# Hash-masked attention and a SwiGLU layer in one kernel: the normed rows of five half batches turned by transposing DMAs

## Chip, core and metric

The kernel runs on one core of a Trainium2 chip. The metric is the device time of one launch in microseconds (us). Of the kernel before, three runs gave 341.06, 342.76 and 345.58 us, a median of 342.76 us.

## What is computed

Four batches, eight heads, 768 tokens, head size 64. Each query and key gets a bucket of six sign bits, a query sees only the keys of its own bucket, and the attention's output (3072 rows of 512) goes through an RMS norm and a SwiGLU layer with 1536 hidden columns.

```python
q_bucket = sum((q @ proj > 0) * 2 ** arange(6)); k_bucket = the same of k
scores   = where(q_bucket == k_bucket, q @ k.T / sqrt(64), -1e9)
attn_out = softmax(scores) @ v                       # 4 x 8 x 768 x 64
x   = attn_out.transpose(0, 2, 1, 3).reshape(3072, 512)
xn  = x / sqrt(mean(x * x) + 1e-6) * rms_g           # rms_g: 512 numbers
g   = xn @ w_gate                                    # 512 x 1536
out = (g * sigmoid(g) * (xn @ w_val)) @ w_out        # 1536 x 512, float32
```

## The kernel before

The work is cut into eight half batches, w = 0 to 7, of 384 rows each, and for the attention into 192 slots: one slot is one third of the keys of one head of one half batch. In slot s the kernel issues the score matmuls of slot s + 1 on TensorE (`scores`, L323) and their exponential on ScalarE (`probs`, L333). Everything else hangs on a hand-written plan: `at(s, f, ..., rank=r)` puts a piece of work into slot s, and within a slot work of rank under 3 comes before the exponential and the rest behind it, in order of rank. No scheduler reorders anything, so each engine does its work in the order of the plan, and an instruction that waits holds up all that stands behind it on its engine.

For a half batch w of 2 or more, the last attention matmul stands in slot end = 24w + 26, and the feed-forward part begins with `g_step` in slot s0 = 24w + 48, which is end + 22. The part in between prepares the rows:

- `attn_out` (L360 to L381): VectorE adds a small mean to the attention output and takes reciprocals, GpSimd multiplies (x) and squares (sq). `sumsq` (L385, VectorE) sums the squares.
- `norm` (L392 to L398), in slot end + 9: VectorE adds the four sums of a row, GpSimd makes 1/sqrt of the mean (rstd).
- `scale_x` (L403), in slots end + 14, 15 and 16, one for each third c of the 384 rows: VectorE multiplies 128 rows of x by rstd and writes them as fp16 (xn).
- `turn_x` (L410, L411), in slots end + 17, 19 and 21: TensorE transposes the 128 rows in four 128x128 pieces into a PSUM bank (x_ps), and VectorE moves the bank to xnT and multiplies by the norm's weight, which lies there as a column (gcol).

Then come, from slot s0 on, twelve pairs of `gate` (L422, TensorE; tanh L424, ScalarE) and `value` (L432, TensorE; L434 and L435, VectorE) in sixteen slots, and `project` (L446) in the nine slots behind them. So while half batch w is being normed, TensorE is at the pairs and the projection of half batch w - 1, and the attention of half batch w + 1 runs through all slots. x_ps, the two banks of a pair, and the projection's bank come from one pool of three PSUM banks (`gps`).

SyncE issues nearly all DMAs, in the order of the plan: the loads of q, k and v of the next heads (L121 in four pieces each for q and k, L111 for v), the moves of the hash bits from SBUF to SBUF (L288, eight for two pairs of heads), and the outputs (L455). The DMAs take eight completion semaphores in turn, so a DMA can't be issued before the one eight places earlier has landed. `v_sum` (L301 to L303, GpSimd) adds the six blocks of v in a scratch tile.

Of the kernel before, what the change touches and what calls it, by code (L numbers as in the profile page):

```python
# [8 lines left out]
FP32 = mybir.dt.float32  # L9
FP16 = mybir.dt.float16  # L10
AF = mybir.ActivationFunctionType
ALU = mybir.AluOpType
# [5 lines left out]
D = 64  # L18
DMODEL = H * D
# [7 lines left out]
KBIT = -32.0  # L27
ESCALE = 1.0 / 8.0
C0 = 1.0e-9

# [11 lines left out]
def kernel(  # L44
# [12 lines left out]
    nc = tc.nc  # L57
    PSUM = bass.MemoryType.PSUM

    const = ctx.enter_context(tc.tile_pool(name="const", bufs=1))  # L60
# [7 lines left out]
    spool = ctx.enter_context(tc.tile_pool(name="spool", bufs=2))  # L68
# [13 lines left out]
    scl = const.tile([128, 1], FP32, name="scl")  # L82
    mhalf = const.tile([128, 3], FP32, name="mhalf")
    gcol = const.tile([128, 4], FP32, name="gcol")
    wg = const.tile([128, 4, DFF], FP16, name="wg")
    wv = const.tile([128, 4, DFF], FP16, name="wv")
    wo = const.tile([128, NF, DMODEL], FP16, name="wo")
    vls = [const.tile([128, H, 6, 66], FP16, name=f"vl{i}") for i in range(2)]
    vsum = [const.tile([128, H, 66], FP16, name=f"vsum{i}") for i in range(2)]
    cvb = [const.tile([128, H, 66], FP32, name=f"cvb{i}") for i in range(2)]  # L90

    def bank(name, shape=None, dt=FP32):
        return gps.tile(shape or [128, 512], dt, name=name, tag="g")
# [203 lines left out]
    def v_sum(b, hp):  # L297
        vn = raw[b, hp, "v"]
        hs = slice(2 * hp, 2 * hp + 2)
        a = spool.tile([128, 2, 3, D], FP32, name="vadd")  # L300
        nc.gpsimd.tensor_add(a, vn[:, :, 0:3], vn[:, :, 3:6])  # L301
        nc.gpsimd.tensor_add(a[:, :, 0], a[:, :, 0], a[:, :, 1])
        nc.gpsimd.tensor_add(vsum[b % 2][:, hs, 0:64], a[:, :, 0], a[:, :, 2])  # L303

    def v_mean(b, hp, n, parts=(None,)):
        hs = slice(2 * hp, 2 * hp + n)
        ps = bank("m_ps", [128, n, 65])
        for i, jt in enumerate(parts):
# [3 lines left out]
            )  # L312
        nc.vector.tensor_scalar_mul(cvb[b % 2][:, hs, 0:65], ps, C0 / S)  # L313


    sps, psb, ot = {}, {}, {}
    x, ssp, xn, xnT, ht = {}, {}, {}, {}, {}
# [70 lines left out]
    rstds = {}  # L388
# [11 lines left out]
    def scale_x(w, c):  # L400
        if w not in xn:
            xn[w] = npool.tile([128, 3, DMODEL], FP16, name="xn")
        nc.vector.tensor_scalar_mul(xn[w][:, c, :], x[w][:, c, :], rstds[w][:, c : c + 1])  # L403

    def turn_x(w, c):
        if w not in xnT:
            xnT[w] = npool.tile([128, 4, HALF], FP16, name="xnT", bufs=2)
        ps = bank("x_ps", [128, 4, 128], FP16)
        for kt in range(4):
            nc.tensor.transpose(ps[:, kt, :], xn[w][:, c, kt * 128 : (kt + 1) * 128], ident16)  # L410
        nc.vector.tensor_mul(  # L411
            xnT[w][:, :, c * 128 : (c + 1) * 128], ps,
            gcol.unsqueeze(2).to_broadcast([128, 4, 128]),
        )
# [88 lines left out]
    def load_wo(f0, f1):  # L503
        nc.gpsimd.dma_start(
            out=wo[:, f0:f1, :],
            in_=moe_w_out[f0 * 128 : f1 * 128, :].rearrange("(k p) n -> p k n", p=128),
        )

    def columns_of_proj():
# [40 lines left out]
    def at(s, f, *a, rank=3):  # L550
        plan[s].append((rank, len(plan[s]), lambda: f(*a)))
# [36 lines left out]
    for i, (t, src) in enumerate(((wg, moe_w_gate), (wv, moe_w_val))):  # L588
        at(2 + 4 * i, load_w, t, src, 0, 768)
        at(12 + 5 * i, load_w, t, src, 768, 1536)  # L590
        at(33 + 6 * i, load_wo, 6 * i, 6 * i + 6)
# [26 lines left out]
    for (b, hp), (loads, turns, cast_slots, sh) in work.items():  # L618
        for which, s in zip("kqv", loads):
            at(s, load_rows if which == "v" else load_blocks, nc.sync, b, hp, which)  # L620
        for i, s in enumerate(turns):
            at(s, turn_dve, b, hp, "kq"[i // 4], i % 4, rank=5)
        for which, s in zip("kq", cast_slots):
            at(s, cast_pool, b, hp, which)
        if sh:
            at(sh, hash_pairs, b, (hp,) if b == 1 else (hp - 1, hp))
        at(cast_slots[2], v_prep, b, hp)
        at(cast_slots[2], v_sum, b, hp)
        if hp % 2:
            at(64 if b == 1 else 48 * b - 4 + 4 * hp, v_mean, b, hp - 1, 4)  # L630
    for hp in range(2):
        at(52 + 4 * hp, v_mean, 1, hp, 2, range(6))

    gts, sqs = {}, {}

    def g_step(w, ft):
# [12 lines left out]
    for w in range(8):  # L649
        for h in range(H):  # L650
            end = LAST[w, h] + 3
            at(end - 1, av, w, h, 0, 9)
            at(end, av, w, h, 9, 18)
            if h % 2:
                at(end, o_step, w, h // 2, rank=4.5)
                if (w, h) != (0, 7):
                    at(end + 6, s_step, w, h // 2, rank=5)
        at(end + (1 if w == 0 else 9), norm, w, rank=5)
        for c in range(3):
            at(end + (3 if w == 0 else 14 + c), scale_x, w, c, rank=5)  # L660
            at(end + (7 + c if w == 0 else 17 + 2 * c), turn_x, w, c, rank=1)
        s0 = 24 * w + 48
        seen = set()
        for ft in range(NF):
            for f, s in ((g_step, s0 + 16 * ft // NF), (v_step, s0 + (32 * ft + 16) // (2 * NF))):
                at(s, f, w, ft, rank=4 if s in seen else 2)
                seen.add(s)
        for i in range(9 if w < 7 else 6):
            c, j = divmod(i, 3)
            at(s0 + 16 + i, project, w, c, 4 * j, 4 * j + 4, rank=1 if i == 8 else 3)  # L670


    for s in range(NS + 48):
# [3 lines left out]
        n = sum(r < 3 for r, _, _ in todo) if s < NS - 1 else 0  # L677
# [54 lines left out]
```

## Time and profile before

| | |
|---|---|
| median of three runs | 342.76 us |
| the profiled execution: its own time | 343.48 us |
| its span in the trace | 341.7 us (1.8 us lie around it) |
| TensorE (PE) busy | 330.2 us, 97% of the span |
| VectorE (DVE) busy | 238.6 us, 70% |
| ScalarE (ACT) busy | 210.2 us, 62% |
| GpSimd (POOL) busy | 150.6 us, 44% |
| granted TensorE clock, mean | 0.995 |

In the lines of the profile, L410 is a line of the kernel before; then come engine, operation, what is written and what is read, with tile sizes, and "x96" is the number of instructions. Behind the bar stand the busy time, the mean of one in nanoseconds, and how long the engine had been idle before them and for whom. PEld is TensorE's loading of weights, which runs beside its matmuls. "SPq" and "POOLq" are queue instructions, the issue of a DMA among them.

### The profile page before, as it was taken

The numbers are of one execution on the slowest core, as the hardware profiler recorded it, in microseconds if no ns is written. First come the engines' busy times: TensorE is split into PE (matmuls) and PEld (weight loads), VectorE is DVE, ScalarE is ACT, GpSimd is POOL, SyncE is SP. The second block draws the span as 40 slices with busy tenths as digits, with TensorE's granted clock in tenths as the row PEclk, the third lists the DMA queues.
The fourth block names the chain that finished last, engine by engine and source line by source line (L and its number), as shares of the span: only waits on it lengthen the run. The fifth ranks groups of instructions, "written<-read, shape, count | busy, mean of one in ns | idle before, by whom it ended". The sixth has DMA issues, their size and how long they took to land.

```text
span 341.7 us, 7760 instructions
## 1 busy us (share of the span) xinstructions
PE 330.2 (97%) x2985; PEld 200.8 (59%) x2985; DVE 238.6 (70%) x530; ACT 210.2 (62%) x328; POOL 150.6 (44%) x222
## 2 busy tenths in 40 slices
PE   8899998999999999999999999999999999999995
PEld 5366665665556565566565666566556655555553
DVE  3577888898759896668668896667446663883860
ACT  3588987756667576657666676567667674322421
POOL 3668897636464667244746475503111311110000
PEclk9899999999999999999999999999999999999999
DMA  6999999635557064507344251100010001002002
GB/s 203 353 175 220 253 186 165 106 84 107 97 148 133 13 107 117 109 17 135 97 101 91 43 115 63 35 16 0 33 63 0 3 2 73 18 2 83 12 0 92
DMA packets 80100, 31.36 MB, mean 92 GB/s; under 512 B 65192, under 2 KB 77120, under 8 KB 80064
## 3 DMA queue, kind: packets, MB, share of 16 engines
q1 hardware_dynamic: 76160, 26.09, 31.1%
q0 software_dynamic: 3680, 4.72, 8.6%
q8 instruction: 23, 0.38, 0.4%
q14 instruction: 13, 0.11, 0.1%
q10 hardware_dynamic: 224, 0.07, 0.1%
HBM read 28.32 MB, written 6.29 MB: 101 GB/s over the span
## 4 chain that ended last, share of the span: by engine, by line
PE 87%; DVE 8%; POOL 1%; issue 1%; ACT 1%; DVEq 0%; ACTq 0%
PE v_ps L432 18%; PE y_ps L446 18%; PE g_ps L422 17%; PE s_ps L323 16%; PE o_ps L345 9%; PE d_ps L209 5%; PE x_ps L410 1%; DVE otmp L360 1%; PE t_ps L169 1%; PE z_ps L491 1%; POOL QK L185 1%; PE y_ps L689 1%; DVE xn L403 1%; DVE ssp L385 1%; PE m_ps L310 1%
## 5 line engine op out<-in xcount | busy, mean ns | idle before, releaser
L333 ACT ACTIVATE psb<-s_ps 128x768 f16<-128x768 f32 x192 | 150.8, 809 | 30.5 <-PE s_ps L323 29.5
L323 PE MATMUL s_ps<-QK 76*128 76x384 f16 x384 | 93.7, 326 | 2.8 <-ACT psb L333 1.1
L424 ACT ACTIVATE t<-g_ps 128x384 f32<-128x384 f32 x96 | 47.2, 492 | 62.2 <-PE g_ps L422 62.0
L432 PE MATMUL v_ps<-xnT,wv 128*128 128x384 f16 x384 | 78.0, 325 | 0.9 <-DVE cvb L313 0.5
L422 PE MATMUL g_ps<-xnT,wg 128*128 128x384 f16 x384 | 78.0, 325 | 0.4 <-DVE xnT L411 0.4
L434 DVE SCALAR_TENSOR_TENSOR a<-t,g_ps 128x384 f32<-128x384 f32 x96 | 52.7, 549 | 27.9 <-ACT t L424 26.1
L446 PE MATMUL y_ps<-wo,ht 128*128 128x512 f16 x276 | 69.2, 378 | 0.5 <-DVE a L434 0.5
L369 POOL TENSOR_TENSOR x<-otmp,rcp 128x384 f32<-128x384 f32 x31 | 25.8, 832 | 95.6 <-DVE rcp L365 95.3
L345 PEld LDWEIGHTS <-psb 128*128 128x128 f16 x1152 | 51.7, 98 | 25.2 <-issue 7.5
L435 DVE SCALAR_TENSOR_TENSOR ht<-a,v_ps 128x384 f16<-128x384 f32 x96 | 53.2, 554 | 11.4 <-PE v_ps L432 2.2
L345 PE MATMUL o_ps<-vl,psb 128*128 128x65 f16 x1152 | 56.8, 193 | 0.4 <-DVE otmp L360 0.4
L432 PEld LDWEIGHTS <-wv 128*128 128x128 f16 x384 | 36.3, 97 | 25.4 <-issue 1.7
L422 PEld LDWEIGHTS <-wg 128*128 128x128 f16 x384 | 35.9, 97 | 24.3 <-issue 0.6
L323 PEld LDWEIGHTS <-QK 76*128 76x128 f16 x384 | 31.6, 98 | 18.5 <-issue 4.9
L446 PEld LDWEIGHTS <-ht 128*128 128x128 f16 x276 | 25.8, 97 | 24.3 <-issue 0.6
L453 ACT COPY ysb<-y_ps 128x512 f32<-128x512 f32 x23 | 13.5, 587 | 25.4 <-PE y_ps L446 22.6
L411 DVE TENSOR_TENSOR xnT<-x_ps,gcol 128x512 f16<-128x512 f16 x24 | 16.3, 685 | 15.9 <-PE x_ps L410 15.9
L381 POOL TENSOR_TENSOR sq<-x 128x384 f32<-128x384 f32 x31 | 25.6, 827 | 2.4
L360 DVE TENSOR_TENSOR otmp<-o_ps,cvb 128x390 f32<-128x390 f32 x32 | 17.9, 558 | 10.3 <-PE o_ps L345 10.3
L201 POOL CAST QK<-kT 64x768 f16<-64x768 f32 x20 | 16.7, 836 | 13.5 <-DVE kT L193 6.5
L216 DVE TENSOR_SCALAR bits<-d_ps,thr,scl 128x384 f16<-128x384 f32 (+1 forms) x20 | 13.3, 675 | 12.4 <-PE d_ps L209 12.3
L201 POOL CAST QK<-qT 64x768 f16<-64x768 f32 x20 | 16.7, 836 | 9.2 <-DVE qT L193 8.6
(74 smaller groups left out, 284.2 us busy)
## 6 DMA issues: line engine op xcount, KB each, us to landing
vL<-in_v_dram SPq DMA_DIRECT2D x16, 384.0 KB
out_dram<-ysb SPq DMA_DIRECT2D x23, 256.0 KB
kL<-in_k_dram SPq DMA_DIRECT2D x40, 96.0 KB
qL<-in_q_dram SPq DMA_DIRECT2D x40, 96.0 KB
kL<-in_k_dram SPq DMA_DIRECT2D x5, 384.0 KB
qL<-in_q_dram SPq DMA_DIRECT2D x5, 384.0 KB
wg<-in_moe_w_gate_dram POOLq DMA_DIRECT2D x2, 768.0 KB, 7.2
wv<-in_moe_w_val_dram POOLq DMA_DIRECT2D x2, 768.0 KB, 9.0
```

Source lines behind the costliest of these rows:

```text
L201: nc.gpsimd.tensor_copy(QK[b, hp][0:64, hh, o : o + S], T0[b, hp, which][64 * hh : 64 * hh + 64, :])
L323: nc.tensor.matmul(ps[:, j, 0:HALF], k_cols(w // 2, h, 2 * p + j), q_cols(w, h), start=True, stop=True,)
L333: nc.scalar.activation(psb[w, h][:, p], sps.pop(g)[:, :, 0:HALF], AF.Exp, scale=ESCALE,)
L345: nc.tensor.matmul(o[:, c, hh, 0:65], psb[w, h][:, jt // 2, jt % 2, 128 * c : 128 * c + 128], vls[b % 2][:, h, v_chunk(b, h, jt), 0:65], s ...
L369: eng.tensor_mul(xd.rearrange("p c (h d) -> p c h d", h=2), tmp[:, :, :, 0:64], r.to_broadcast([128, 3, 2, 64]),)
L381: nc.gpsimd.tensor_mul(sq, xd, xd)
L422: nc.tensor.matmul(g, wg[:, kt, fs], xnT[w][:, kt], start=(kt == 0), stop=(kt == 3))
L424: nc.scalar.activation(t, g, AF.Tanh, scale=0.5)
L432: nc.tensor.matmul(vv, wv[:, kt, fs], xnT[w][:, kt], start=(kt == 0), stop=(kt == 3))
L434: nc.vector.scalar_tensor_tensor(out=a, in0=t, scalar=1.0, in1=g, op0=ALU.add, op1=ALU.mult)
L435: nc.vector.scalar_tensor_tensor(out=ht[w][:, ft], in0=a, scalar=0.5, in1=vv, op0=ALU.mult, op1=ALU.mult)
L446: nc.tensor.matmul(y, ht[w][:, ft, c * 128 : (c + 1) * 128], wo[:, ft, :], start=(ft == 0), stop=(ft == NF - 1),)
```

## The change

Half batches 2 to 6 no longer use TensorE for the turn. VectorE multiplies x by rstd and by the norm's weight in one instruction, for which the weight is loaded once as a row copied to all partitions (grow). Then SyncE issues twelve transposing DMAs for each of these half batches, each 128x128 fp16 from xn to xnT. In their plan `norm` stands in slot end + 7, and `scale_x` and `turn_x` of third c both in slot end + 11 + c, the latter at rank 6, behind the slot's other work. Half batches 0, 1 and 7 are as before. `v_sum` forms its sum in a smaller scratch tile, which with one buffer instead of two makes room for grow.

```diff
+BY_DMA = (2, 3, 4, 5, 6)
+    grow = const.tile([128, DMODEL], FP32, name="grow")
 def v_sum(b, hp):
-        a = spool.tile([128, 2, 3, D], FP32, name="vadd")
-        nc.gpsimd.tensor_add(a, vn[:, :, 0:3], vn[:, :, 3:6])
-        nc.gpsimd.tensor_add(a[:, :, 0], a[:, :, 0], a[:, :, 1])
-        nc.gpsimd.tensor_add(vsum[b % 2][:, hs, 0:64], a[:, :, 0], a[:, :, 2])
+        a = spool.tile([128, 2, 2, D], FP32, name="vadd", bufs=1)
+        nc.gpsimd.tensor_add(a, vn[:, :, 0:2], vn[:, :, 2:4])
+        nc.gpsimd.tensor_add(a, a, vn[:, :, 4:6])
+        nc.gpsimd.tensor_add(vsum[b % 2][:, hs, 0:64], a[:, :, 0], a[:, :, 1])
 def scale_x(w, c):
-        nc.vector.tensor_scalar_mul(xn[w][:, c, :], x[w][:, c, :], rstds[w][:, c : c + 1])
+        if w in BY_DMA:
+            nc.vector.scalar_tensor_tensor(
+                out=xn[w][:, c, :], in0=x[w][:, c, :], scalar=rstds[w][:, c : c + 1],
+                in1=grow, op0=ALU.mult, op1=ALU.mult,
+            )
+        else:
+            nc.vector.tensor_scalar_mul(xn[w][:, c, :], x[w][:, c, :], rstds[w][:, c : c + 1])
 def turn_x(w, c):
+        if w in BY_DMA:
+            for kt in range(4):
+                nc.sync.dma_start(
+                    out=xnT[w][:, kt, c * 128 : (c + 1) * 128],
+                    in_=xn[w][:, c, kt * 128 : (kt + 1) * 128], transpose=True,
+                )
+            return
+    def load_grow():
+        nc.sync.dma_start(
+            out=grow, in_=moe_rms_g.rearrange("(o n) -> o n", o=1).to_broadcast([128, DMODEL])
+        )
+    at(63, load_grow)
-        at(end + (1 if w == 0 else 9), norm, w, rank=5)
+        at(end + (1 if w == 0 else 7 if w in BY_DMA else 9), norm, w, rank=5)
         for c in range(3):
-            at(end + (3 if w == 0 else 14 + c), scale_x, w, c, rank=5)
-            at(end + (7 + c if w == 0 else 17 + 2 * c), turn_x, w, c, rank=1)
+            scale, turn, rank = (3, 7 + c, 1) if w == 0 else (14 + c, 17 + 2 * c, 1)
+            if w in BY_DMA:
+                scale, turn, rank = 11 + c, 11 + c, 6
+            at(end + scale, scale_x, w, c, rank=5)
+            at(end + turn, turn_x, w, c, rank=rank)
```

## The prediction

> **What bounds the kernel now.** I read the page's first part, then the waits, then the timeline around one turn.
>
> ```profile
> PE 330.2 (97%) x2985; PEld 200.8 (59%) x2985; DVE 238.6 (70%) x530; ACT 210.2 (62%) x328; POOL 150.6 (44%) x222
> PE 87%; DVE 8%; POOL 1%; issue 1%; ACT 1%; DVEq 0%; ACTq 0%
> ```
>
> TensorE is busy 97% of the span and makes 87% of the chain that ended last. Between 58 and 290 us the view of the waits gives it 1.4 us of waiting in all. So what shortens the kernel is TensorE work taken away, and what lengthens it is any wait of TensorE. VectorE, ScalarE, GpSimd and SyncE have room on the average, but the room at the places touched must be read there. The timeline of TensorE at the projection of half batch 2:
>
> ```profile
> 166.12 0.49 PE L323 MATMUL s_ps<-QK 76*128 76x384 f16 x2
> 166.44 1.03 PE L446 MATMUL y_ps<-wo,ht 128*128 128x512 f16 x4
> 167.31 0.49 PE L323 MATMUL s_ps<-QK 76*128 76x384 f16 x2
> 167.63 0.39 PE L410 MATMUL x_ps<-ident,xn 128*128 128x128 f16 x4
> 167.86 1.03 PE L446 MATMUL y_ps<-wo,ht 128*128 128x512 f16 x4
> ```
>
> Columns: start, duration (us). Matmuls overlap, so the cost of a turn is read from starts: without one, y_ps starts 0.32 us after s_ps; with one, 0.55 us after it. A turn of four transposes costs TensorE 0.23 us, though the groups give L410 9.3 us for 96.
>
> **What goes.** Five half batches of three turns: 15 x 0.23 = 3.4 us of TensorE. The chain, which holds x_ps at 1.4% of the span (4.8 us for 24 turns), gives 15/24 of it, 3.0 us. I take 3.4. The built order confirms 60 weight loads and 60 matmuls fewer on TensorE. VectorE loses 15 evictions:
>
> ```profile
> L411 DVE TENSOR_TENSOR xnT<-x_ps,gcol 128x512 f16<-128x512 f16 x24 | 16.3, 685 | 15.9 <-PE x_ps L410 15.9
> L403 DVE TENSOR_SCALAR xn<-x,rstd 128x512 f16<-128x512 f32 x24 | 14.8, 652 | 0.0
> ```
>
> 15 x 0.685 = 10.3 us, off the path, and 15 uses of the three PSUM banks, for which TensorE hardly waits.
>
> **What the scaling costs.** It gets a second SBUF input. Rows of the same operation: 279 ns for 128 columns (L376), 553 for 384 (L434), so 1.07 ns per column and 0.69 us for 512, against 0.65 now: 0.6 us over 15, and VectorE gains 9.7 in all. But it moves three slots forward, from the projection's slots into the last pairs. There VectorE is nearly full: 7.26 of the 8 us from 118 to 126. For half batch 2:
>
> ```profile
> 122.05 0.55 DVE L434 SCALAR_TENSOR_TENSOR a<-t,g_ps 128x384 f32<-128x384 f32 x1
> 122.71 0.55 DVE L435 SCALAR_TENSOR_TENSOR ht<-a,v_ps 128x384 f16<-128x384 f32 x1
> ```
>
> The first projection's matmul starts at 124.59 and takes the bank that this L435 leaves at 123.26; with three banks the slack is 1.3 us. The value matmul before it, at 123.61, takes the bank of this L434, left at 122.60: 1.0 us. Two of three scalings come ahead by then, 1.4 us, less 0.3 us that VectorE idled. So TensorE waits 0 to 0.4 us. Half batch 3 shows the same pairs (161.5 to 163.5), 4 is alike, and in 5 and 6 VectorE idles 0.4 to 0.95 us between pairs. I take 0.8 us in all; nothing if the slack holds, 3 x 2.07 = 6.2 us if all three scalings reach TensorE each time.
>
> GpSimd: `v_sum` was 996 + 458 + 457 ns. At (996 - 458)/256 = 2.1 ns per column, 256 columns take 0.73 us, and 0.73 + 0.73 + 0.46 is the same 1.9. The norm two slots earlier finds GpSimd idle (2.1 us before L394 at 120.00). grow is one more issue at slot 63 (0.34 to 0.71 us by the rows below), 22 slots ahead of its first use.
>
> **What the transposing DMAs cost.** No row shows one. Two numbers matter: I, how long one keeps SyncE (or the rings) before the next goes, and L, its landing. SyncE's own rows give medians for I of 338 ns (outputs), 492 (v), 644 (pieces of q and k) and 714 (bits). The upper end is far: the longest single issue of a piece took 2,513. The bits are the nearest, the only moves from SBUF to SBUF, so I take 0.71. L, from timelines of SyncE and GpSimd:
>
> ```profile
> 117.53 3.20 SPq L288 DMA_DIRECT2D QK<-bits  x4
> 120.83 2.69 SPq L121 DMA_DIRECT2D kL<-in_k_dram  x4
> 123.57 2.71 SPq L121 DMA_DIRECT2D qL<-in_q_dram  x4
> ...
> 122.08 1.70 POOL L201 CAST QK<-kT 64x768 f16<-64x768 f32 x2 [0.93 <-DMA QK<-bits]
> ```
>
> The last bits are issued by 120.73 and release GpSimd at 122.08: L = 1.35, taken as 1.4 (first load of the trace, from HBM: 2.9).
>
> Now the cover, half batch by half batch, in times of the trace before, with the gate 0.68 us earlier (three turns less). Half batch 2: the scores of slot 85 start at 120.13, but SyncE is late: it had waited for the bits, and the q pieces that the plan puts ahead of the transposes go out until 126.28. The gate starts at 137.36 - 0.68 = 136.68. So 136.68 - 126.28 - 1.4 = 9.0 us are left for twelve issues: 12 x 0.71 = 8.5 fits, by half a microsecond, and I = 0.75 is the limit. For the others the start is the first scaling's end, or SyncE's freedom if later (161.8; 198.9 plus a v load of 0.64; 237.4; 273.9), the gates 176.26, 214.34, 252.67 and 288.48, less 0.68: covers of 12.4, 12.7, 13.2 and 12.5 us, limits of I of 1.03 to 1.1. The last scaling comes at least 8 slots ahead of the gate and its four transposes follow it, so it doesn't bind. If the cover fails, TensorE stands for 12 I minus the cover, each time.
>
> Behind the transposes on SyncE wait v loads (for half batch 2 needed 12 slots later, at slot 100), outputs and pieces of q and k of slots 90 to 98. A delay of 8.5 us leaves the pieces ahead of their turns on VectorE in slot 106. The output of slot 90 goes out some 6 us later, and with two ysb buffers ScalarE's third copy may wait under 1 us, once; I leave it at nothing, since ScalarE idles 62 us before the tanh. The eight semaphores bind only if a landing takes over 8 x 0.71 = 5.7 us.
>
> **Sum.** -3.4 + 0.8 + 0 = -2.6 on the profiled execution's own 343.48: 340.9 us, -0.8%. The median of the runs is 0.7 lower than that execution, within their spread of 4.5, so I shift nothing.
>
> **A rule against it.** The trace moves a SBUF-to-SBUF piece every 0.71 us. The Trainium skill, "VectorE: DVE Perf Modes", section "The three transpose paths", gives 1309 ns for a 128x128 transpose by DMA and 390 by TensorE, and advises TensorE where PSUM will do; no run here shows that figure. By it, I = 1.31, the waits would be an estimated 6.7 + 3.3 + 3.0 + 2.5 + 3.2 = 18.7 us and the time 359.6, within the second case of the first rival below. "Advanced Engine Details and Errata", section "X-Bar Transpose (TRN2)", says instead that such DMAs are as fast as regular ones, which agrees with my choice.
>
> **Rivals.**
> *Transposes too slow for the cover* (slower). From I = 0.75 half batch 2 waits, from 1.03 the others too. With I twice the bits' row, 1.43, 12 I = 17.1 and the waits are 8.1 + 4.7 + 4.4 + 3.9 + 4.6 = 25.7: 366.6 us. With 2.51, 30.2: 91 us, 432. It passes +2% (349.6) at about I = 1.14. For it: 65,192 of the 80,100 DMA packets are under 512 B and rows of 256 B are such, and the rings are busy 0.84 to 1.06 from 123 to 129 us, just ahead of the first transposes. Against it: they are idle from 131 to 134 and the dearest median row is 0.71. Chance of I between 0.75 and 1.14: 0.12 (341 to 349.6); to 1.43: 0.14 (to 366.6); above: 0.14.
> *VectorE becomes the bound in the last pairs of half batches 2 to 4*: up to 6.2 - 3.4 = +2.8, 346.3 us. For it the 91% there, against it the slack of 1.0 to 1.3 us. 0.07.
> *More gain than the transposes themselves*: to pass -2% it would take 6.9 us, and TensorE's waits outside the first 10 us hold too little. 0.03.
> *Nothing is moved*: excluded by the built order.
>
> **Numbers.** The forecast, with 338.5 to 343.5 of its own, has 0.50. 2% is about what a measurement of this kernel tells from no change. Within it: 0.50 + 0.12 + 0.07 = 0.69; slower 0.28; faster 0.03. The range goes from 338.5 to 366 and leaves out the slowest rival and the fast one, 0.17.
>
> **What would show it.** The DMA issues on SyncE in the timeline: a time per transpose near 0.7 and an end before the gate. The waits: g_ps L439 of TensorE waiting for DMA xnT at zero or only for half batch 2. xn near 0.69 us each. The starts of y_ps in projections without x_ps 0.32 behind s_ps. Wrong would make me a wait of TensorE for xnT in every half batch, or VectorE's L451 and L452 holding up TensorE around 122, 162 and 199 us.

## The result, and the profile after

The changed kernel takes 371.91 us (median of six runs, 369.58 to 376.13) against 341.59 for the kernel before (median of six runs, the three above among them): a ratio of 1.0846, 95% interval 1.0799 to 1.0894. It is slower by 29 us by the ratio and by 30.3 by the medians, where 2.6 us of gain were forecast; it lies beyond the range of 338.5 to 366. Its profiled execution took 375.52 us and is one of two in six that ran about 4 us longer than the rest, so its sums are some 4 us too large.

The first and fourth part of the page of the changed kernel (busy time by engine, and the chain by engine and line):

```profile
PE 342.9 (92%) x2925; PEld 201.3 (54%) x2925; DVE 232.3 (62%) x515; ACT 209.9 (56%) x328; POOL 152.3 (41%) x222
...
PE 62%; SPq 16%; DVE 11%; DMA 4%; issue 2%; ACT 2%; POOL 1%; DVEq 0%; ACTq 0%
PE g_ps L439 15%; PE v_ps L449 15%; SPq L420 15%; PE s_ps L327 10%; PE y_ps L463 7%; PE o_ps L349 7%; PE d_ps L213 4%; DMA out_dram<-ysb 2%; DVE otmp L364 1%; DMA xnT<-xn 1%; DVE xn L408 1%; DVE a L451 1%; DVE kT L197 1%; PE t_ps L173 1%; DMA qL<-in_q_dram 1%
```

TensorE fell from 97% to 92% of a longer span, and a new member is in the chain: SyncE's issue of the transposing DMAs, L420, with 15% of the span, 56 us. TensorE also has 60 matmuls less and yet 12.7 us more of busy time; the same matmuls took longer. SyncE's own timeline at half batch 2, and the answer on line L420 (durations in ns: least, median, most):

```profile
123.98 0.64 SPq L125 DMA_DIRECT2D qL<-in_q_dram  x1
124.73 15.75 SPq L420 DMA_TRANSPOSE xnT<-xn  x12
140.53 0.58 SPq L115 DMA_DIRECT2D vL<-in_v_dram  x1
141.21 0.88 SPq L472 DMA_DIRECT2D out_dram<-ysb  x2
```

```profile
L420 SPq DMA_TRANSPOSE xnT<-xn x60: 1099/1230/2410, 124.7 to 316.6; - x60
```

Twelve issues keep SyncE for 15.75 us, 1.31 each, and the v load and two outputs wait behind them. What TensorE and ScalarE make of that, from their timelines:

```profile
134.14 1.03 PE L463 MATMUL y_ps<-wo,ht 128*128 128x512 f16 x4
137.88 0.32 PE L439 MATMUL g_ps<-xnT,wg 128*128 128x384 f16 x1 [2.72 <-DMA xnT<-xn]
139.12 0.48 PE L439 MATMUL g_ps<-xnT,wg 128*128 128x384 f16 x1 [0.92 <-DMA xnT<-xn]
140.38 0.50 PE L439 MATMUL g_ps<-xnT,wg 128*128 128x384 f16 x1 [0.78 <-DMA xnT<-xn]
141.63 0.50 PE L439 MATMUL g_ps<-xnT,wg 128*128 128x384 f16 x1 [0.75 <-DMA xnT<-xn]
...
145.61 1.44 PE L439 MATMUL g_ps<-xnT,wg 128*128 128x384 f16 x4 [0.66 <-ACT ysb L470]
```

```profile
189.77 0.58 ACT L470 COPY ysb<-y_ps 128x512 f32<-128x512 f32 x1 [8.06 <-DMA out_dram<-ysb]
```

The gate could have begun at 135.0. Its four matmuls come 1.25 us apart instead, as the last four transposes land one by one. Then TensorE waits for ScalarE, and a group of four gate matmuls takes 1.44 us where it takes 0.81 elsewhere. Ahead of half batch 3's first gate ScalarE stood 8.06 us at the copy of an output, because both buffers (ysb) were still held by outputs behind the transposes. Over the whole run (us in all, times, longest):

```profile
ACT ysb L470 <- DMA out_dram<-ysb: 20.2, 3, 8.1
```

The busy times around half batch 2's first gate show the third effect (PEclk is the granted clock):

```profile
132.00:138.00 6.00, 3.28 (x32) 1.83 (x31) 0.56 (x2) 1.16 (x2) 3.27 (x5) 1.00 0.12 23
138.00:144.00 6.00, 3.03 (x9) 0.95 (x8) 0.43 (x1) 0.00 (x0) 0.00 (x0) 0.55 0.43 125
144.00:150.00 6.00, 5.34 (x35) 2.87 (x34) 3.00 (x7) 3.68 (x6) 0.00 (x0) 0.59 0.99 204
150.00:156.00 6.00, 6.00 (x60) 3.23 (x58) 4.60 (x10) 2.76 (x5) 5.04 (x7) 1.00 0.14 23
```

Columns: the window, its length, the busy time of PE, PEld, DVE, ACT and POOL, then PEclk, the DMA engines' share and GB/s. Once TensorE has idled, the mean clock is 0.55 and 0.59 in the next two windows. So there are three candidates for the loss: the waits for xnT, the slower clock behind them, and the outputs held on SyncE.

### The profile page after: what moved, and what is told of

Its sections match the earlier page's. It is cut to its first block, busy times and chain, and to the rows that moved or that the text cites. A ratio compares the mean times of both kernels' runs of the same rounds, so it can differ in the third digit from the quotient of the medians.

```text
span 373.7 us, 7711 instructions
## 1 busy us (share of the span) xinstructions
PE 342.9 (92%) x2925; PEld 201.3 (54%) x2925; DVE 232.3 (62%) x515; ACT 209.9 (56%) x328; POOL 152.3 (41%) x222
## 4 chain that ended last, share of the span: by engine, by line
PE 62%; SPq 16%; DVE 11%; DMA 4%; issue 2%; ACT 2%; POOL 1%; DVEq 0%; ACTq 0%
PE g_ps L439 15%; PE v_ps L449 15%; SPq L420 15%; PE s_ps L327 10%; PE y_ps L463 7%; PE o_ps L349 7%; PE d_ps L213 4%; DMA out_dram<-ysb 2%; DVE otmp L364 1%; DMA xnT<-xn 1%; DVE xn L408 1%; DVE a L451 1%; DVE kT L197 1%; PE t_ps L173 1%; DMA qL<-in_q_dram 1%
## 5 line engine op out<-in xcount | busy, mean ns | idle before, releaser
L439 PE MATMUL g_ps<-xnT,wg 128*128 128x384 f16 x384 | 85.6, 341 | 18.2 <-DMA xnT<-xn 14.2
L327 PE MATMUL s_ps<-QK 76*128 76x384 f16 x384 | 96.3, 334 | 2.3 <-ACT psb L337 1.1
L449 PE MATMUL v_ps<-xnT,wv 128*128 128x384 f16 x384 | 82.3, 338 | 2.1 <-ACT ysb L470 1.4
L373 POOL TENSOR_TENSOR x<-otmp,rcp 128x384 f32<-128x384 f32 x31 | 26.9, 867 | 132.4 <-DVE rcp L369 132.3
L349 PEld LDWEIGHTS <-psb 128*128 128x128 f16 x1152 | 53.2, 99 | 27.0 <-issue 10.2
L439 PEld LDWEIGHTS <-wg 128*128 128x128 f16 x384 | 37.0, 100 | 48.3 <-DMA xnT<-xn 14.8
L349 PE MATMUL o_ps<-vl,psb 128*128 128x65 f16 x1152 | 58.2, 196 | 0.4 <-DVE otmp L364 0.2
L449 PEld LDWEIGHTS <-wv 128*128 128x128 f16 x384 | 37.5, 100 | 28.9 <-issue 6.9
L470 ACT COPY ysb<-y_ps 128x512 f32<-128x512 f32 x23 | 13.5, 585 | 52.7 <-DMA out_dram<-ysb 20.2
L463 PEld LDWEIGHTS <-ht 128*128 128x128 f16 x276 | 26.3, 97 | 26.2 <-issue 0.6
L197 DVE STREAM_TRANSPOSE qT<-qL 128x192 f32<-128x192 f32 x40 | 19.5, 519 | 0.0
```

What stands on the lines that cost most here:

```text
L327: nc.tensor.matmul(ps[:, j, 0:HALF], k_cols(w // 2, h, 2 * p + j), q_cols(w, h), start=True, stop=True,)
L349: nc.tensor.matmul(o[:, c, hh, 0:65], psb[w, h][:, jt // 2, jt % 2, 128 * c : 128 * c + 128], vls[b % 2][:, h, v_chunk(b, h, jt), 0:65], s ...
L373: eng.tensor_mul(xd.rearrange("p c (h d) -> p c h d", h=2), tmp[:, :, :, 0:64], r.to_broadcast([128, 3, 2, 64]),)
L439: nc.tensor.matmul(g, wg[:, kt, fs], xnT[w][:, kt], start=(kt == 0), stop=(kt == 3))
L449: nc.tensor.matmul(vv, wv[:, kt, fs], xnT[w][:, kt], start=(kt == 0), stop=(kt == 3))
L463: nc.tensor.matmul(y, ht[w][:, ft, c * 128 : (c + 1) * 128], wo[:, ft, :], start=(ft == 0), stop=(ft == NF - 1),)
```

## The experiments

**The rest of the change, without the DMAs.**

```diff
 def turn_x(w, c):
-        if w in BY_DMA: (four transposing DMAs)
         ps = bank("x_ps", ...); four nc.tensor.transpose
+        if w in BY_DMA:
+            nc.vector.tensor_copy(xnT[w][:, :, c * 128 : (c + 1) * 128], ps)
+            return
-                scale, turn, rank = 11 + c, 11 + c, 6
+                scale = 11 + c
```

> All of the change but the transposing DMAs: scaling with the weight row in slots end + 11 to 13, grow loaded, the small scratch tile, and the turn on TensorE as before (slots end + 17, 19, 21) with a plain move out of the bank. Theory (the loss is the transposing DMAs: twelve issues of 1.31 us on SyncE outlast the cover): TensorE's waits for xnT are gone, 341.6 as before, within 341 to 343. Rival (the scaling moved into the full last pairs, or the new row, costs a part): 344 or more, with TensorE waiting for VectorE near the last pairs.

342.64 us against 341.81, ratio 1.0042 (1.0001 to 1.0083). Of the loss of 29 us, the scaling in the full slots, the row of weights and the new scratch tile hold at most 2.8. The scaling is dearer than forecast, and TensorE doesn't wait for it:

```profile
L408 DVE SCALAR_TENSOR_TENSOR xn<-x,rstd,grow 128x512 f16<-128x512 f32 x15 | 12.4, 825 | 0.0
```

**A third of the transposes.**

```diff
+DMA_THIRDS = {(w, 0) for w in BY_DMA}
-        if w in BY_DMA:          # in scale_x, turn_x and the plan
+        if (w, c) in DMA_THIRDS:
```

> Only the first third (c = 0) of half batches 2 to 6 goes by DMA, the other two are turned on TensorE as in the kernel before. Theory: four issues of 1.31 us = 5.2 us fit every cover (9.0 to 13.2 us), so no wait for xnT, and 5 turns x 0.23 us = 1.1 us of TensorE are saved: about 340.5. Rival (any transposing DMA disturbs the rings or SyncE, in proportion to its count): a third of the loss of 30 us, about 351.

340.91 against 341.81, ratio 0.9977 (0.9959 to 0.9996): a small gain, no third of the loss. Four issues take SyncE 4.9 to 5.9 us, inside every cover, and no wait for xnT is left. Transposing DMAs do no harm by being there; they harm once the last one outlasts its cover.

**TensorE kept busy while it waits.**

```diff
+FILL = {2: 44, 3: 32, 4: 34, 5: 22, 6: 24}
         g = bank("g_ps", [128, HALF])
+        for _ in range(FILL.get(w, 0) if ft == 0 else 0):
+            nc.tensor.matmul(g, ones16, wg[:, 0, 0:HALF], start=True, stop=True)
```

> The changed kernel, with matmuls on constants (44, 32, 34, 22 and 24 of 384 columns, about 0.16 us each) into the gate's own bank ahead of the first gate of half batches 2 to 6, so that TensorE is busy while it waits for xnT. The waits themselves (about 20 us by the profile) stay. Theory (the rest of the loss is the clock, granted at about 0.55 for some 8 to 12 us behind each wait): the clock stays near 1.0 and the time falls by 10 to 13 us, to 359 to 362. Rival (the rest is the held outputs, or the slow clock is no consequence of the waiting): it stays at 370 or more, or rises.

370.09 us, and the clock at 0.994: the expected fall didn't come, and the time is the one that the rival named. This doesn't clear the clock. The 156 matmuls take 26.2 us, more than the waits, and they end where the next hindrance begins: TensorE then waits 4.0 us in all, 2.6 at the longest, for ScalarE's copies of held outputs. The run mixes all three causes, and the following ones had to part them.

**One issue for a third of the rows.**

```diff
         if w in BY_DMA:
-            for kt in range(4):
-                nc.sync.dma_start(
-                    out=xnT[w][:, kt, c * 128 : (c + 1) * 128],
-                    in_=xn[w][:, c, kt * 128 : (kt + 1) * 128], transpose=True,
-                )
+            nc.sync.dma_start(
+                out=xnT[w][:, :, c * 128 : (c + 1) * 128], in_=xn[w][:, c, :], transpose=True,
+            )
```

> The changed kernel, but one transposing DMA of 128x512 for each third in place of four of 128x128: 3 issues for each half batch, the same bytes. Theory A (the time belongs to the issue, whatever its size): 3 x 1.3 = 3.9 us fit every cover, 371.9 falls to 341.6 - 3.4, about 338 to 340. Theory B (the time belongs to the 128x128 piece, or to its bytes): one takes 4 x 1.3 = 5.2 us and the kernel stays at 368 to 374.

338.35 against 341.81, ratio 0.9933 (0.9901 to 0.9964): Theory A. The answer on that line, and SyncE's timeline at half batch 2:

```profile
L419 SPq DMA_TRANSPOSE xnT<-xn x15: 1190/1198/1682, 124.1 to 273.3; - x15
```

```profile
124.14 3.94 SPq L419 DMA_TRANSPOSE xnT<-xn  x3
128.13 0.58 SPq L115 DMA_DIRECT2D vL<-in_v_dram  x1
```

A transposing DMA of 128x512 keeps SyncE 1.198 us, one of 128x128 1.230. The same bytes in a quarter of the issues take 3.94 us and not 15.75, TensorE waits for no xnT, and the granted clock stays at 0.999. The gain is 3.5 us by the medians and 2.3 (1.2 to 3.4) by the ratio. It has the price of the scaling in it; the forecast for that sum was 2.6.

**Outputs from ScalarE's queue.**

```diff
-            nc.sync.dma_start(out=rows[:, out_chunk(w, c), :], in_=ysb)
+            nc.scalar.dma_start(out=rows[:, out_chunk(w, c), :], in_=ysb)
```

> The changed kernel with the outputs of project issued by ScalarE, right behind its copy, and no longer by SyncE behind the transposes. Filling TensorE's waits kept the clock at 0.994 and yet gave 370.1, with TensorE waiting 2.6 and 0.9 us for ScalarE's copy of an output. Theory (the held outputs cost a part of their own, behind the waits for xnT): 371.9 falls by 3 to 6 us, to 366 to 369. Rival (the outputs are hidden by the waits for xnT and the slow clock): 370 to 373.

386.45 us, 14.5 more than the changed kernel, against both expectations. TensorE's waits for ScalarE's copies are gone, but its waits for xnT rise from 14.2 to 34.5 us, since the transposes now stop on SyncE:

```profile
SPq L420 <- DMA out_dram<-ysb: 6.5, 1, 6.5
```

(SyncE's waits between 120 and 150 us: in total, times, longest.) Twelve issues take 21.6 us in place of 15.75. The trace shows why. The eight completion semaphores go round over the DMAs of both engines, and the third transpose of half batch 2 has the same one as the output that ScalarE issues at 131.19. That output lands at 133.24, and the transpose goes out at 133.26, 6.5 us after the second was done:

```profile
124.22 2.50 SPq L420 DMA_TRANSPOSE xnT<-xn  x2
131.19 0.34 ACTq L472 DMA_DIRECT2D out_dram<-ysb  x1
133.26 3.64 SPq L420 DMA_TRANSPOSE xnT<-xn  x3
```

So this run says nothing on the price of a held output.

**The same with TensorE kept busy**, 36, 21, 24, 11 and 14 matmuls.

> As the run before it, and TensorE kept busy ahead of the first gates, with fewer matmuls than in the first such run: 36, 21, 24, 11 and 14 (17.3 us in all; the 156 there took 26.2 us and outlasted the waits of 19.9 us). Theory (slow clock behind the waits is a cost of its own): 341.6 - 3.4 + about 20 = 358 to 360, and 8 us or more below the run without the fill. Rival (the clock costs nothing by itself): within 2 us of the run without the fill.

387.63 us, within the 2 us of the run before it that the rival names. But the waits of that run are twice as long as this fill: TensorE still waited 19.8 us for xnT, and the clock stayed down, at 0.963. So this is inconclusive too.

**Smaller pieces.**

```diff
+PIECES = {3: 64, 4: 32}          # rows in one DMA; 128 elsewhere, first third only
+                nr = PIECES.get(w, 128)
+                for r in range(0, 128, nr):
+                    nc.sync.dma_start(out=xnT[w][:, kt, c * 128 + r : c * 128 + r + nr],
+                        in_=xn[w][r : r + nr, c, kt * 128 : (kt + 1) * 128], transpose=True)
```

> Only the first third of half batches 2 to 6 goes by DMA; in half batch 3 in pieces of 64 rows (8 issues), in 4 in pieces of 32 rows (16 issues), in 2, 5 and 6 in pieces of 128x128 (4). Measured is the time from issue to issue. Theory A (the time belongs to the issue): 1.2 us for every size, so half batch 4 takes 16 x 1.2 = 19 us and TensorE waits for it. Theory B (to the bytes, with a floor that only the 128x512 escapes): 0.6 and 0.3 us.

SyncE's timeline, half batches 2, 3 and 4:

```profile
126.93 6.40 SPq L424 DMA_TRANSPOSE xnT<-xn  x4
...
161.46 10.02 SPq L424 DMA_TRANSPOSE xnT<-xn  x8
...
199.35 20.50 SPq L424 DMA_TRANSPOSE xnT<-xn  x16
```

From issue to issue, pieces of 64 rows take 1.25 us and of 32 rows 1.28; the issues by themselves have medians of 1.226 and 1.224 us. With 128x512 at 1.198, one issue costs the same over a sixteenfold range of bytes. Half batch 4 outlasts its cover again, and the single time is 354.83 us.

**Seven half batches with one issue for each third.**

```diff
-BY_DMA = (2, 3, 4, 5, 6)
+BY_DMA = (1, 2, 3, 4, 5, 6, 7)
-    at(63, load_grow)
+    at(44, load_grow)
```

> One transposing DMA of 128x512 for each third, now for half batches 1 to 7, with grow loaded in slot 44. Theory: two half batches more, 6 turns x 0.23 = 1.4 us less than the same for 2 to 6 (338.35): about 337. Rival (half batch 7's gates come sooner, since no attention runs beside them, and half batch 1's issue stands behind bits and loads on SyncE): 338.5 or more with TensorE waiting for xnT at one of the two.

341.36 us, ratio 0.9976 (0.9957 to 0.9996): the rival's number, but not its cause. Nothing waits for xnT. TensorE's waits between 58 and 100 us:

```profile
PE y_ps L461 <- DVE a L449: 2.2, 1, 2.2
```

This is the prediction's second rival, VectorE full in the last pairs, at a half batch where it was not looked for: at 1, VectorE makes hash bits (1.31 us) and scales the first third (0.66 us) ahead of the last pair but one, and scales the other two (1.21 us) ahead of the last pair, whose bank TensorE waits for.

**Three output buffers.** Then the remaining causes were parted, with ysb in three buffers. The room for the third comes from leaving out the norm's weight in half batches 2 to 6:

```diff
-            ysb = spool.tile([128, DMODEL], FP32, name="ysb")
+            ysb = spool.tile([128, DMODEL], FP32, name="ysb", bufs=3)
-    grow = const.tile([128, DMODEL], FP32, name="grow")
-    at(63, load_grow)
-        if w in BY_DMA: scalar_tensor_tensor with grow
+        nc.vector.tensor_scalar_mul(xn[w][:, c, :], x[w][:, c, :], rstds[w][:, c : c + 1])
```

> The changed kernel with three buffers for the output rows (ysb) in place of two, so that ScalarE's third copy of a half batch need not wait until SyncE has issued the first output behind the transposes. The room comes from leaving out grow: the norm's weight is not applied in half batches 2 to 6. Theory (outputs held behind the transposes cost a part of their own): TensorE's 5 us of waiting for ScalarE's copies are gone and the time falls from 371.9 to 365 to 368. Rival (that waiting lies in the shadow of the waits for xnT and the slow clock): 370 to 373.

361.34 us, 10.6 below the changed kernel and below either expectation. No copy of an output waits for a buffer any more. By this pair the held outputs cost about 10 us, twice the 4.9 us that the waits of TensorE put down to them; leaving out grow also spares VectorE 0.2 us a scaling, which the first run bounds at 2.8 us together with the rest of the change.

The 361.34 is no sharp figure: the four runs took 358.21, 359.34, 363.34 and 363.58 us, at clocks of 0.986, 0.981, 0.972 and 0.972. The profiled one is the third. In it TensorE waits for hash bits at 37.6 us, long before the first transpose, and the mean clock is 0.56 from 42 to 45 us:

```profile
PE s_ps L326 <- DMA QK<-bits: 2.6, 1, 2.6
```

The wait and the slow clock behind it cost some 4 us that have nothing to do with the transposes. Whether the run of 363.58 has the same isn't shown. If so, this kernel takes about 359 us, and the held outputs cost some 13.

**Three output buffers and TensorE kept busy**, with 40, 21, 24, 16 and 23 matmuls.

> As the run before it, with matmuls on constants ahead of the first gates, 40, 21, 24, 16 and 23 of 0.163 us, 20.2 us in all, counted from the first such run to end where the twelfth transpose lands. Theory (the slow clock behind each wait is a cost of its own): clock near 1.0 and 341.6 - 3.4 + 21 = 358 to 361. Rival (it costs nothing by itself): within 2 us of the run before it.

358.48 us, clock 1.0. The first part of its page:

```profile
PE 345.7 (97%) x3049; PEld 208.8 (58%) x3049; DVE 227.9 (64%) x515; ACT 210.0 (59%) x328; POOL 150.1 (42%) x222
```

345.7 us less 124 x 0.163 = 20.2 us of constants is 325.5, and the run with one issue has 324.6: apart from the constants the two do the same work in the same time, and they lie 20.1 us apart (358.48 and 338.35). So wait and slow clock together cost 23.0 us by the medians (361.34 - 338.35) and some 20 by the two faster runs without constants; the constants win back 2.9 net (361.34 - 358.48), or 0.3 against those two. The constants are a little longer than the waits they fill. In the timeline of TensorE without them, from the moment at which the first gate matmul could start to the start of what follows the four, half batches 2 to 6 take 7.2, 3.8, 4.0, 2.4 and 3.0 us where four matmuls in a row take 0.65. That is 17.1 us of waiting in all, 3.1 less than the constants. So the wait for xnT costs 17 us (at most 20), and the slow clock behind it 3 to 6, less than the 10 to 13 us that expectations gave it. The timeline of the run without constants, at half batch 4:

```profile
225.73 1.03 PE L456 MATMUL y_ps<-wo,ht 128*128 128x512 f16 x4
226.73 0.32 PE L432 MATMUL g_ps<-xnT,wg 128*128 128x384 f16 x1
227.89 0.34 PE L432 MATMUL g_ps<-xnT,wg 128*128 128x384 f16 x1 [0.84 <-DMA xnT<-xn]
229.16 0.34 PE L432 MATMUL g_ps<-xnT,wg 128*128 128x384 f16 x1 [0.93 <-DMA xnT<-xn]
230.43 0.34 PE L432 MATMUL g_ps<-xnT,wg 128*128 128x384 f16 x1 [0.94 <-DMA xnT<-xn]
230.60 0.28 PE L313 MATMUL m_ps<-vsum,ones 128*128 128x260 f16 x1
```

The output's four matmuls end their 0.86 us of issue at 226.60, and 230.60 is 4.0 us later.

**Two output buffers and the same fill.**

> The changed kernel with the same matmuls on constants and two ysb buffers as it has. The first such run gave 370.1 with 26.2 us of them, some 4 to 5 us more than the waits. If the slow clock and the held outputs each cost a part: 370.1 - 5 = 364 to 367, above the run with three buffers by 4 to 6. If the clock costs nothing: 370 or more.

369.16 us (366.5 to 372.0), above what was expected. Against three buffers it is 10.7 us longer, against the changed kernel 2.8 shorter. The other pairing gave 10.6 and 2.9; with runs that spread over 5 us, so close an agreement is partly luck. The two profiled executions, 366.50 and 358.81 us, say what a held output costs. Their spans differ by 7.7 us. In the one TensorE waits 5.7 us longer for ScalarE's copies than in the other, and it is busy 347.7 us against 345.7, at clocks of 0.994 and 1.000. So to the wait comes a slower clock, and the held outputs cost 8 to 13 us, depending on the pair.

**One issue for each third, half batches 2 to 7.**

> One transposing DMA of 128x512 for each third, for half batches 2 to 7. With 1 too it gave 341.4, with TensorE waiting 3 us for VectorE near half batch 1's last pairs, and no wait for xnT. Theory (half batch 1 alone spoiled it): 338.35 - 0.7 = 337.7, within 336.5 to 339. Rival (half batch 7 is at fault): 340 or more.

338.28 against 342.15, ratio 0.9877 (0.9854 to 0.9899). It beats both kernels, by about 1% and 9%. Half batch 7 adds nothing that can be told from the run with 2 to 6, and half batch 1 was what spoiled the run with all seven.

## Why the prediction was wrong

**What bounds the kernel, and what the whole is worth without waits: right.** The forecast was 3.4 us for 15 turns less 0.8 for the scaling, a gain of 2.6; with the waits out of the way it is 3.5 by the medians and 2.3 by the ratio. No run has the turns' 3.4 by themselves.

**The scaling: right in its place, off in its size.** 0.825 us an instruction measured, 0.69 forecast from two rows of the same operation; the whole rest of the change 1.4 us (0 to 2.8) where 0.8 was taken. In half batches 2 to 4 TensorE waited for VectorE 0.5 us, once, as it does in the kernel before, and not for a scaling.

**The issue of a transposing DMA, I: the step that failed.** "The bits are the nearest, the only moves from SBUF to SBUF, so I take 0.71." It measured 1.23 us by itself and 1.31 in a row. At 0.75 the cover of half batch 2 was gone, at 1.03 to 1.1 the others. The view of SyncE before the change held issues of 0.34 to 0.71 us by the kind of access pattern, and a new kind of instruction was priced by where its data lies. The covers themselves were read well: the first rival's sum at I = 1.31, 18.7 us, stands against 17 to 20 in the runs that isolate it. That rival had the mechanism, with a chance of 0.14 for I from 1.14 to 1.43, and its sign, a wait for xnT in every half batch, came. The time lies above its 366.6 because it left out what the sum left out too, the two terms that follow.

The trace thus decides between the two sentences of the Trainium skill that the prediction weighed. "VectorE: DVE Perf Modes", section "The three transpose paths", gives 1309 ns for a 128x128 DMA transpose, and the trace has 1.31 us from issue to issue. "As fast as regular DMAs" ("Advanced Engine Details and Errata", section "X-Bar Transpose (TRN2)") isn't borne out for the time of an issue: it is 1.23 us against 0.34 to 0.71, though one of 128x512 takes no longer.

**The outputs behind the transposes: left at nothing, cost about 10 us (8 to 13).** The prediction looked at half batch 2 alone, at 8.5 us of delay, and said that ScalarE "idles 62 us before the tanh". That idle time is ScalarE waiting for gate matmuls, and is no room: each half batch has three outputs in the nine slots ahead of the next gate, two buffers are used up at the third, and the copy that waits for a buffer stands ahead of the first tanh, without which the pairs' banks don't come free.

**The clock was no term of the sum**: 3 to 6 us behind the waits for xnT, 20 to 23 together with them, and a part of what the held outputs cost.

From kernel to kernel the medians go from 341.81 (before) to 338.35 (one issue), 361.34 (three buffers) and 371.91 (the change): -3.5, +23.0 and +10.6. Such steps always add up to the whole, so their sum is no check on them, and each of the last two is open by some 3 us.

## What to carry to other kernels

Before a step moves to a queue, price one issue of the very instruction that is added, and if no trace has it, take the range's dear end as a case of its own: a cover of 9 us for twelve issues is a bet on 0.75 us each. If the cost belongs to the issue, ask first for fewer and larger ones; here the same bytes in a quarter of the issues turned 8% of loss into 1% of gain. And count what stands behind the new issues on the queue together with the buffers of its producers: an engine that copies into two buffers is held at the third. A DMA moved to another engine's queue isn't out of the way either, as long as it shares completion semaphores with the DMAs left behind.

## What the runs showed of the hardware

- A transposing DMA from SBUF to SBUF on SyncE kept it 1.20 us for 128x512 fp16 and 1.23, 1.23 and 1.22 for pieces of 128, 64 and 32 rows by 128 (medians): a time of the issue and not of the bytes.
- In the changed kernel the clock fell near 138.7 us, with TensorE idle from 135.0 but for one matmul at 137.88, and came back near 148.9; TensorE's last wait had ended at 145.61. "TensorE: Matmul & The Clock Gate" of the Trainium skill, Part 1, says that the clock halves after about 3.4 us of idleness and returns after as much sustained work. The trace agrees, with 0.50 for the level (columns as above) and some 3.3 us of work for the return:

```profile
138.00:140.00 2.00, 0.68 (x2) 0.00 (x0) 0.00 (x0) 0.00 (x0) 0.00 (x0) 0.66 0.15 31
146.00:148.00 2.00, 2.00 (x16) 1.15 (x15) 1.90 (x5) 1.57 (x3) 0.00 (x0) 0.50 0.95 219
148.00:150.00 2.00, 2.00 (x18) 1.20 (x17) 1.08 (x3) 1.08 (x2) 0.00 (x0) 0.78 0.94 146
```

- In this program a DMA waits for the landing of the one that had its completion semaphore before it, whichever engine issued that one: with the outputs issued by ScalarE, a transpose on SyncE stood 6.5 us and went out 0.02 us after an output's landing.
